# Output weights in 4 KB rows for four heads, and the last value load split in two, in a decode attention kernel

## The chip, the cores and the metric

The kernel runs on one core of one Trainium2 chip. The time is device microseconds of one execution, given as a median over runs. The profile is one execution recorded by the hardware profiler; its span (first to last instruction) is 1.5 to 1.9 us below the time. Landing times, start times and the durations of single DMA packets that the text quotes are records of the same traces.

## The reference, cut to what matters

Two attention layers decode one token for a batch of four; the results are put side by side. Part A has 8 key and value heads and looks at the last 2048 positions; part B has 32 heads and looks at the whole cache of 8192.

```python
def _B_ref(x, k_cache, v_cache, wq, wo):      # part A: the same, with a window and shared heads
    B, Sq, D = x.shape                        # 4, 1, 512
    H, Dh = 32, 128
    q = (x @ wq).reshape(B, Sq, H, Dh) ...    # transposed to heads
    scores = einsum("bhqd,bhkd->bhqk", q, k_cache) * Dh ** -0.5
    p = softmax(scores)
    o = einsum("bhqk,bhkd->bhqd", p, v_cache)
    return o ... .reshape(B, Sq, H * Dh) @ wo # wo: 4096 x 512, 4 MB in bf16
```

Keys and values of part B are 537 MB of the 587 that have to be read. Part B's output weights `wo` are only 4 MB.

## The kernel before: the parts that matter

Part B goes in 64 chunks: two heads of one batch element, 4 MB of keys and 4 MB of values. Each key tile is transposed on TensorE (into `tr`), copied to SBUF (`kt`), multiplied with the query (`sc`); the value tiles are multiplied with the probabilities (`po`). Two chunks are a "pair" here: their results are scaled (`oz`), brought into the row order of the weights by products with selection masks (into `ms`), cast (`zB`), and multiplied with the weights (`fin`).

The weights of two heads are one load, in rows of 2 KB, because partition p holds rows 2p and 2p+1:

```python
LASTV = (64, 32, 16, 8, 8)
...
def dma_wos(hp):
    src = B_wo[2 * hp * P:2 * (hp + 1) * P, :].rearrange("(p r) n -> p (r n)", r=2)
    sch.add_dma("sp", lambda e: e.dma_start(wos[:, :, :].rearrange("p r n -> p (r n)"), src), "d_wos",
                waits=[("fin", NCA + 4 * hp - 1)] if hp else [], key=("wos", hp))
```

The very last pair takes a shorter way from `po` to the result: its weights are turned back into plain row order beforehand, by products with `back2` masks, so that `oz` can be multiplied directly. The last chunk's values (128 tiles, 4 MB) arrive in pieces by `LASTV`:

```python
def emit_wol():
    for u in range(2):
        o = tr[:, u, :].bitcast(F32)
        for r in range(2):
            pe_mm(o, back2[:, u, r, :], wos[:, r, :], start=r == 0, stop=r == 1, ...)
        ...                                    # one copy on ScalarE, one on VectorE, into wol
...
norm_sum(NC - 1)                               # the end of the program
for g in range(chunks[NC - 1]["NG"]):
    emit_pv(NC - 1, g)                         # 8 value tiles each
    if g == LASTV[0] // TG - 1:
        emit_wol()                             # after the first 64 tiles
pv_done(NC - 1)
emit_fin(NC - 1)
```

## Time and profile before

| | before |
|---|---|
| time, median of 3 runs | 1374.14 us (1374.09 to 1374.22) |
| span of the profile | 1372.6 us |
| loads of part B's output weights | 16 of 256 KB, 2048 packets of 2 KB |
| values of the chunk before the last land at | 1359.160 us |
| last value load lands at | 1369.060 us |
| last value product starts at | 1369.326 us |

First, the end of the chain of work that ended last (start, duration, what). It says that the last value load was what TensorE waited for last:

```profile
1329.92 39.14 DMA kv<-in_B_v_cache_dram
1369.06 0.05 issue
1369.11 0.42 PE po L410 x8
```

Second, from the timeline, TensorE's wait (in brackets) for the values of the chunk before the last; third, from the table of waits, all its waits for part B's keys (sum in us, times, longest):

```profile
1359.21 0.64 PE L410 MATMUL po<-pbb,kv 128*128 128x64 bf16 x16 [0.46 <-DMA kv<-in_B_v_cache_dram]
```

```profile
PE tr L408 <- DMA kv<-in_B_k_cache_dram: 141.5, 58, 4.1
```

From 1359.21 on TensorE has work without a pause until the last pieces of the last chunk. So the stretch from the landing of those values to the last value product, 1369.326 - 1359.160 = 10.166 us, is a good measure of the end: what the queue gained or lost earlier does not enter into it. I call it **the end stretch** below. For everything ahead of it I use **the body**: from the landing of the very first load to the landing of those values, 1359.160 - 13.290 = 1345.870 us.

### The profile page before, as it was taken

What the parts mean: (1) busy time and instruction counts of PE and PEld (TensorE: products, weight loads), DVE (VectorE), ACT (ScalarE), POOL (GpSimd) and SP (SyncE); (2) the same over time, 40 slices, a digit from 0 to 9 for tenths busy, and PEclk for the clock granted to TensorE, in tenths of its full rate; (3) what the DMA queues carried; (4) which work ended last, traced back from release to release, by engine and by line L of the source; (5) the groups of instructions that cost most, each with busy time, mean ns of one, the idle gap of its engine ahead of it and who ended that gap; (6) DMA issues with size and microseconds to landing.
All of it is one profiled execution on the core that took longest, in us unless ns stands there. A gap on an engine that the chain in (4) does not pass through costs nothing.

```text
span 1372.6 us, 59967 instructions
## 1 busy us (share of the span) xinstructions
PE 1176.5 (86%) x27065; PEld 1132.9 (83%) x27067; DVE 656.6 (48%) x1434; ACT 434.7 (32%) x650; POOL 7.3 (1%) x28
## 2 busy tenths in 40 slices
PE   4888898889888888988888888888898888888888
PEld 4777898888888888888888878888898888888888
DVE  1775454445444444454445444444454444444544
ACT  1553232333223322332233323322333233323322
POOL 2000000000000000000000000000000000000000
PEclk9998999999999999999999999999999999999999
DMA  9999999999999999999999999999999999999998
GB/s 400 423 424 432 429 433 428 433 432 432 432 431 433 429 434 428 434 430 434 430 434 430 430 433 432 432 431 433 429 433 431 434 429 434 430 432 432 432 427 352
DMA packets 25261, 587.53 MB, mean 428 GB/s; under 512 B 2820, under 2 KB 2840, under 8 KB 6296
## 3 DMA queue, kind: packets, MB, share of 16 engines
q1 hardware_dynamic: 25208, 587.22, 99.8%
q8 instruction: 16, 0.26, 0.1%
q14 instruction: 5, 0.04, 0.0%
q10 hardware_dynamic: 32, 0.01, 0.0%
HBM read 587.21 MB, written 0.01 MB: 428 GB/s over the span
## 4 chain that ended last, share of the span: by engine, by line
DMA 65%; PE 33%; issue 1%; DVE 1%; ACT 0%; SPq 0%; DVEq 0%
DMA kv<-in_B_k_cache_dram 57%; PE tr L408 21%; PE sc L410 9%; DMA kv<-in_A_k_cache_dram 5%; DMA kv<-in_B_v_cache_dram 3%; PE po L410 2%; PE fin L410 1%; PE ms L410 0%; ACT kt L476 0%; DVE sA L527 0%; SPq L365 0%; ACT pba L597 0%; PE ms L408 0%; DVE zA L683 0%; DVE rm L536 0%
## 5 line engine op out<-in xcount | busy, mean ns | idle before, releaser
L408 PE MATMUL tr<-identb,kv 128*128 128x128 bf16 x8704 | 697.9, 230 | 148.8 <-DMA kv<-in_B_k_cache_dram 141.5
L478 DVE COPY kt<-tr 128x1024 bf16<-128x1024 bf16 x736 | 502.6, 690 | 457.1 <-PE tr L408 452.7
L408 PEld LDWEIGHTS tr<-identb,kv 128*128 128x128 bf16 x8704 | 552.9, 104 | 165.2 <-DMA kv<-in_B_k_cache_dram 81.7
L476 ACT ACTIVATE kt<-tr 128x1024 bf16<-128x1024 bf16 x352 | 359.3, 1023 | 666.8 <-PE tr L408 666.7
L410 PE MATMUL sc<-qb,kt 128*128 128x64 bf16 x8704 | 446.2, 196 | 14.3 <-ACT kt L476 12.8
L410 PEld LDWEIGHTS sc<-qb,kt 128*128 128x128 bf16 x8704 | 366.4, 100 | 26.0 <-ACT kt L476 20.2
L410 PE MATMUL po<-pbb,kv 128*128 128x64 bf16 x8320 | 284.4, 192 | 4.5 <-issue 3.9
L410 PEld LDWEIGHTS po<-pbb,kv 128*128 128x128 bf16 x8320 | 263.2, 97 | 7.1 <-issue 4.1
L577 ACT ACTIVATE pbb<-sc,negb 64x128 bf16<-64x128 f32 x128 | 51.6, 403 | 254.3 <-DVE negb L564 253.5
L541 DVE TENSOR_REDUCE rm<-sc 64x1 f32<-64x128 f32 x128 | 37.0, 289 | 56.6 <-PE sc L410 55.7
L553 DVE TENSOR_REDUCE gm<-ms 1x2 f32<-1x128 f32 (+1 forms) x72 | 20.1, 279 | 48.4 <-PE ms L408 48.4
L564 DVE COPY negb<-ms 128x1 f32<-128x1 f32 (+1 forms) x72 | 11.4, 158 | 47.0 <-PE ms L410 46.8
L410 PE MATMUL ms<-identf,gx 1*128 1x1 f32 (+1 forms) x144 | 27.2, 256 | 0.8 <-DVE zA L683 0.8
L666 DVE TENSOR_TENSOR oz<-po,rz 128x8 bf16<-128x8 f32 x33 | 5.5, 166 | 40.7 <-PE po L410 40.7
L410 PEld LDWEIGHTS ms<-identf,gx 1*128 1x128 f32 (+1 forms) x144 | 21.1, 182 | 4.6 <-DVE zA L683 0.9
L577 ACT ACTIVATION_READ_ACCUMULATOR pbb<-sc,negb 64x1 f32 x128 | 23.7, 185 | 0.0
L410 PE MATMUL po<-pba,kv 128*128 128x64 bf16 x512 | 20.5, 199 | 3.5 <-issue 2.1
L410 PEld LDWEIGHTS po<-pba,kv 128*128 128x128 bf16 x512 | 17.9, 102 | 5.7 <-ACT pba L597 4.2
L408 PE MATMUL ms<-identf,rm 128*1 128x128 f32 (+1 forms) x72 | 19.5, 271 | 2.4 <-DVE rm L536 2.3
L557 DVE TENSOR_SCALAR gx<-gm 1x128 f32<-1x128 f32 (+1 forms) x72 | 16.0, 222 | 2.5
L683 DVE CAST zB<-ms 64x8 bf16<-64x8 f32 x64 | 10.5, 164 | 9.2 <-PE ms L410 8.7
L410 PE MATMUL ms<-xT,kv 128*128 128x4 bf16 x256 | 7.1, 166 | 8.8 <-DMA kv<-in_A_wq_dram 5.0
(61 smaller groups left out, 173.9 us busy)
## 6 DMA issues: line engine op xcount, KB each, us to landing
kv<-in_B_k_cache_dram SPq DMA_DIRECT2D x63, 4096.0 KB, 26.5
kv<-in_B_v_cache_dram SPq DMA_DIRECT2D x63, 4096.0 KB, 30.9
kv<-in_A_k_cache_dram SPq DMA_DIRECT2D x8, 2048.0 KB, 14.8
kv<-in_A_v_cache_dram SPq DMA_DIRECT2D x8, 2048.0 KB, 16.2
kv<-in_A_wq_dram SPq DMA_DIRECT2D x1, 4096.0 KB, 12.5
kv<-in_B_wq_dram SPq DMA_DIRECT2D x1, 4096.0 KB, 27.1
wor<-in_A_wo_dram SPq DMA_DIRECT2D x8, 512.0 KB, 9.8
wos<-in_B_wo_dram SPq DMA_DIRECT2D x16, 256.0 KB, 20.3
```

Of the source, the lines that this page charges most:

```text
L408: sch.add("pe", lambda e: e.transpose(o, l, r), waits, key)
L410: sch.add("pe", lambda e: e.matmul(o, l, r, start=start, stop=stop), waits, key)
L476: sch.add("act", lambda e: e.activation(dst, src, ACTF.Copy), waits=waits, key=("ev", s))
L478: sch.add("dve", lambda e: e.tensor_copy(dst, src), waits=waits, key=("ev", s))
L541: sch.add("dve", lambda e, src=src, pp=pp: e.tensor_reduce(out=rm[pp, m, 0:1], in_=src, axis=AX.X, op=ALU.max), waits=[("S", ch["s_last"]) ...
L553: sch.add("dve", lambda e: e.tensor_reduce(out=gm[0:C, m, 0:U], in_=src, axis=AX.X, op=ALU.max), waits=[("trm", c)], key=("gmax", c))
L557: sch.add("dve", lambda e: e.tensor_scalar(out=dst, in0=gv, scalar1=-scale, scalar2=None, op0=ALU.mult), waits=[("gmax", c)], key=("gx", c))
L564: sch.add("dve", lambda e: e.tensor_copy(negb[:, m, 0:C], ms[:, col:col + C]), waits=[("bc", c)], key=("negb", c))
L577: sch.add("act", lambda e, src=src, pp=pp, n=n, u=u: e.activation(probs_of(c)[pp, :, u], src, ACTF.Exp, bias=negb[pp, m, 0:1], scale=scale ...
L666: sch.add("dve", lambda e: e.tensor_tensor(out=o, in0=i0, in1=i1, op=ALU.mult), waits=waits, key=("oT", c))
L683: sch.add("dve", lambda e, src=src, pp=pp: e.tensor_copy(z[pp, :].rearrange("p (r b) -> p r b", r=k), src), waits=[("sm", c)] + free if h ...
```

## The change

The intent: rows of 4 KB mean half as many packets for the weights, and half as many loads; with the last 256 KB of values in two loads, four value products instead of eight have to follow the very last landing. The price is that a load now serves four heads, that is two pairs of heads, so each pair's work runs over four rows per partition. The core of the diff (cut: comments, mask tables, loop constants, the places of the loads in the queue):

```diff
-LASTV = (64, 32, 16, 8, 8)
+LASTV = (64, 32, 16, 8, 4, 4)
...
-        def dma_wos(hp):
+        def dma_wos(hq):
-            src = B_wo[2 * hp * P:2 * (hp + 1) * P, :].rearrange("(p r) n -> p (r n)", r=2)
+            src = B_wo[4 * hq * P:4 * (hq + 1) * P, :].rearrange("(p r) n -> p (r n)", r=4)
...                                   # emit_sel
-            for r in range(k):                      # k = 2, n = 8 in part B
-                pe_mm(ms[:, Z0 + r * n:Z0 + (r + 1) * n], sel[:, r, :], x,
+            for r in range(4):
+                pe_mm(ms[:, Z0 + r * 16:Z0 + (r + 1) * 16], sel4[:, r, :], x,
...                                   # emit_wol
-                for r in range(2):
-                    pe_mm(o, back2[:, u, r, :], wos[:, r, :], start=r == 0, stop=r == 1,
+                for r in range(4):
+                    pe_mm(o, back4[:, u, r, :], wos[:, r, :], start=r == 0, stop=r == 3,
...                                   # emit_fin
-                ops = [(zB[:, r * NB:(r + 1) * NB], wos[:, r, :]) for r in range(2)]
+                ops = [(zB[:, r * NB:(r + 1) * NB], wos[:, r, :]) for r in range(4)]
```

More of the change, by code (lines that the diff above doesn't have):

```diff
@@ L216, in bass_concat_heads__sliding_block_cached__mha_block_cached__decode_kernel @@
         kt = sb("kt", [P, NKT, TG * P], BF16)
-        wos = sb("wos", [P, 2, DO], BF16)
+        wos = sb("wos", [P, 4, DO], BF16)
         qb = sb("qb", [P, 2, NW], BF16)
@@ L236, in bass_concat_heads__sliding_block_cached__mha_block_cached__decode_kernel @@
         rinv = sb("rinv", [P, NSM, 16], F32)
-        rz = sb("rz", [P, 8], F32)
-        pm = sb("pm", [P, HB // 2 + 1, 2, 2, 4], F32)
+        rz = sb("rz", [P, 16], F32)
+        pm = sb("pm", [P, HB + 2, 2, 2, 4], F32)
         pbt = {0: sb("pba", [P, NPB, NTA * 16 + NW], BF16), 1: sb("pbb", [P, NPB, NTB * 2 + NW], BF16)}
         oT = sb("oT", [P, NSM, 16], BF16)
-        oz = sb("oz", [P, 8], BF16)
+        oz = sb("oz", [P, 16], BF16)
         outsb = sb("outsb", [36, DO], BF16)
@@ L244, in bass_concat_heads__sliding_block_cached__mha_block_cached__decode_kernel @@
         sel4 = sb("sel4", [P, 4, P], BF16)
-        sel2 = sb("sel2", [P, 2, P], BF16)
-        back2 = sb("back2", [P, 2, 2, P], BF16)
+        back4 = sb("back4", [P, 2, 4, P], BF16)
         zA = sb("zA", [P, 2, 16], BF16)
-        zB = sb("zB", [P, 8], BF16)
+        zB = sb("zB", [P, 16], BF16)
         wol = sb("wol", [P, 2, DO], BF16)
@@ L279, in bass_concat_heads__sliding_block_cached__mha_block_cached__decode_kernel @@
         sch.add("pool", lambda e: e.memset(pm[:, :, :, :, :], 0.0), key="c_pm0")
-        for x in range(2):
-            sch.add("pool", lambda e, x=x: e.memset(pm[:, 1:, x, x, :], 1.0), waits=["c_pm0"], key="c_pm" if x else None)
+        for i in range(4):
+            sch.add("pool", lambda e, i=i: e.memset(pm[:, 2 + i::4, i // 2, i % 2, :], 1.0), waits=["c_pm0"], key="c_pm" if i == 3 else None)
         sch.add("pool", lambda e: e.memset(pbt[0][:, :, :], 0.0), key=("c_pb", 0))
@@ L290, in bass_concat_heads__sliding_block_cached__mha_block_cached__decode_kernel @@
                 fill=0.0, base=-r, channel_multiplier=1), waits=["c_onesb"])
-        for r in range(2):
-            sch.add("pool", lambda e, r=r: e.affine_select(
-                out=sel2[:, r, :], in_=onesb[:, :], pattern=[[0, 2], [-2, 64]], compare_op=ALU.is_equal,
-                fill=0.0, base=-r, channel_multiplier=1))
+        for r in range(4):
             for u in range(2):
                 sch.add("pool", lambda e, r=r, u=u: e.affine_select(
-                    out=back2[:, u, r, :], in_=onesb[:, :], pattern=[[1, P]], compare_op=ALU.is_equal,
-                    fill=0.0, base=P * u - r, channel_multiplier=-2), key="c_sel" if r == u == 1 else None)
+                    out=back4[:, u, r, :], in_=onesb[:, :], pattern=[[1, P]], compare_op=ALU.is_equal,
+                    fill=0.0, base=2 * P + P * u - r, channel_multiplier=-4), key="c_sel" if r == 3 and u == 1 else None)
         half_of = {}
@@ L334, in dma_wo @@
                         waits=[("fin", g - 2)] if g >= 2 and slot < 2 else [], key=("wo", g))
-        def dma_wos(hp):
-            src = B_wo[2 * hp * P:2 * (hp + 1) * P, :].rearrange("(p r) n -> p (r n)", r=2)
+        def dma_wos(hq):
+            src = B_wo[4 * hq * P:4 * (hq + 1) * P, :].rearrange("(p r) n -> p (r n)", r=4)
             sch.add_dma("sp", lambda e: e.dma_start(wos[:, :, :].rearrange("p r n -> p (r n)"), src), "d_wos",
-                        waits=[("fin", NCA + 4 * hp - 1)] if hp else [], key=("wos", hp))
+                        waits=[("fin", NCA + 8 * hq - 1)] if hq else [], key=("wos", hq))
         def dma_kv(kind, c):
@@ L387, in bass_concat_heads__sliding_block_cached__mha_block_cached__decode_kernel @@
         for kind, c in loads:
-            if kind == "k" and c >= NCA and (c == NCA or (c - NCA) % 4 == 3 and c > NCA + 3):
-                dma_wos((c - NCA) // 4)
+            if kind == "k" and c >= NCA and (c == NCA or (c - NCA) % 8 == 3 and c > NCA + 3):
+                dma_wos((c - NCA) // 8)
             dma_kv(kind, c)
             if kind == "v" and c > NCA and (c - NCA) % 2 == 1:
-                hp = max(0, c - NCA - 2) // 4
-                sch.add("sp", lambda e: e.sem_inc(sems["eng_sp"], 1), waits=[("wos", hp)] + (["kl"] if c == NC - 1 else []),
+                hq = max(0, c - NCA - 2) // 8
+                sch.add("sp", lambda e: e.sem_inc(sems["eng_sp"], 1), waits=[("wos", hq)] + (["kl"] if c == NC - 1 else []),
                         key=("wos2", c - 2 if c > NCA + 1 else NONE), self_inc=True)
@@ L398, in bass_concat_heads__sliding_block_cached__mha_block_cached__decode_kernel @@
                 dma_wo(c)
-        sch.add("sp", lambda e: e.sem_inc(sems["eng_sp"], 1), waits=[("wos", HB // 2 - 1)], key=("wos2", NC - 1), self_inc=True)
+        sch.add("sp", lambda e: e.sem_inc(sems["eng_sp"], 1), waits=[("wos", HB // 4 - 1)], key=("wos2", NC - 1), self_inc=True)
         ms_read = []
@@ L646, in norm_sum @@
             if c >= NCA or c == NONE:
-                pair = 4 * (c - NCA - 1 + 4) if c != NONE else 8
+                pair = 16 * ((c - NCA - 1) // 2 + 2) if c != NONE else 16
                 pv = pm[:, :, :, :, :].rearrange("p a b c d -> p (a b c d)")
                 sch.add("dve", lambda e, x=0: e.tensor_tensor(
-                    out=rz[:, :].rearrange("p (x y) -> p x y", x=2), in0=bcast(ri, [[0, 2], [1, 4]]),
-                    in1=pv[:, bass.ds(x + pair, 8)].rearrange("p (x y) -> p x y", x=2), op=ALU.mult),
+                    out=rz[:, :].rearrange("p (x y) -> p x y", x=4), in0=bcast(ri, [[0, 4], [1, 4]]),
+                    in1=pv[:, bass.ds(x + pair, 16)].rearrange("p (x y) -> p x y", x=4), op=ALU.mult),
                     waits=[("rinv", c), "c_pm"], key=("rz", c), at=pair)
@@ L661, in norm_out @@
             else:
-                o, i0 = oz[:, :].rearrange("p (x y) -> p x y", x=2), bcast(po[:, 0:4], [[0, 2], [1, 4]])
-                i1 = rz[:, :].rearrange("p (x y) -> p x y", x=2)
+                o, i0 = oz[:, :].rearrange("p (x y) -> p x y", x=4), bcast(po[:, 0:4], [[0, 4], [1, 4]])
+                i1 = rz[:, :].rearrange("p (x y) -> p x y", x=4)
             waits = [("rinv" if 0 <= c < NCA else "rz", c), ("pv", c)] + ([("sm", c - 2 if c != NCA + 1 else NONE)] if c >= 2 else [])
@@ L671, in emit_sel @@
             if 0 <= c < NCA:
-                sel, x, n, z, k = sel4, oT[:, c % NSM, :], 16, zA[:, c % 2, :], 4
+                x, z, order = oT[:, c % NSM, :], zA[:, c % 2, :], "p (r b h) -> p h r b"
                 free = [("fin", c - 2)] if c >= 2 else []
             else:
-                sel, x, n, z, k = sel2, oz[:, :], 8, zB[:, :], 2
+                x, z, order = oz[:, :], zB[:, :], "p (r s b u) -> p s u r b"
                 free = [("fin", c - 2 if c - 2 >= NCA else NONE)] if c != NONE else []
-            for r in range(k):
-                pe_mm(ms[:, Z0 + r * n:Z0 + (r + 1) * n], sel[:, r, :], x,
-                      waits=[("oT", c)] + ms_read if r == 0 else [], key=("sm", c) if r == k - 1 else None)
-            for h in range(k):
-                pp = slice(h * P // k, (h + 1) * P // k)
-                src = ms[pp, Z0:Z0 + k * n].rearrange("p (r b h) -> p h r b", r=k, b=NB)[:, h]
-                sch.add("dve", lambda e, src=src, pp=pp: e.tensor_copy(z[pp, :].rearrange("p (r b) -> p r b", r=k), src),
-                        waits=[("sm", c)] + free if h == 0 else [], key=("z", c) if h == k - 1 else None)
+            for r in range(4):
+                pe_mm(ms[:, Z0 + r * 16:Z0 + (r + 1) * 16], sel4[:, r, :], x,
+                      waits=[("oT", c)] + ms_read if r == 0 else [], key=("sm", c) if r == 3 else None)
+            for h in range(4):
+                pp = slice(h * P // 4, (h + 1) * P // 4)
+                if 0 <= c < NCA:
+                    src = ms[pp, Z0:Z0 + 64].rearrange(order, r=4, b=NB)[:, h]
+                else:
+                    src = ms[pp, Z0:Z0 + 64].rearrange(order, r=4, s=2, b=NB)[:, h // 2, h % 2]
+                sch.add("dve", lambda e, src=src, pp=pp: e.tensor_copy(z[pp, :].rearrange("p (r b) -> p r b", r=4), src),
+                        waits=[("sm", c)] + free if h == 0 else [], key=("z", c) if h == 3 else None)
             ms_read[:] = [("z", c)]
@@ L690, in emit_wol @@
                 o = tr[:, u, :].bitcast(F32)
-                for r in range(2):
-                    pe_mm(o, back2[:, u, r, :], wos[:, r, :], start=r == 0, stop=r == 1,
-                          waits=[("wos2", NC - 1)] if u == r == 0 else [], key=("back", u) if r else None)
+                for r in range(4):
+                    pe_mm(o, back4[:, u, r, :], wos[:, r, :], start=r == 0, stop=r == 3,
+                          waits=[("wos2", NC - 1)] if u == r == 0 else [], key=("back", u) if r == 3 else None)
                 if u == 0:
@@ L701, in emit_fin @@
             if c == NC - 1:
-                ov = oz[:, :].rearrange("p (b u) -> p b u", u=2)
+                ov = oz[:, 8:16].rearrange("p (b u) -> p b u", u=2)
                 ops = [(ov[:, :, u], wol[:, u, :]) for u in range(2)]
```

## The prediction

> **What bounds the kernel now.** I read the page first, for the busy shares and the DMA row; then the queue and issue tables; then the chain of work that ended last, in the steady part; then the end of the timeline.
>
> ```profile
> PE 1176.5 (86%) x27065; PEld 1132.9 (83%) x27067; DVE 656.6 (48%) x1434; ACT 434.7 (32%) x650; POOL 7.3 (1%) x28
> DMA  9999999999999999999999999999999999999998
> DMA packets 25261, 587.53 MB, mean 428 GB/s; under 512 B 2820, under 2 KB 2840, under 8 KB 6296
> q1 hardware_dynamic: 25208, 587.22, 99.8%
> ...
> DMA 65%; PE 33%; issue 1%; DVE 1%; ACT 0%; SPq 0%; DVEq 0%
> ...
> wor<-in_A_wo_dram SPq DMA_DIRECT2D x8, 512.0 KB, 9.8
> wos<-in_B_wo_dram SPq DMA_DIRECT2D x16, 256.0 KB, 20.3
> ```
>
> The load queue's packets fill 99.8% of the 16 engines' span. No engine of the core comes near that: TensorE is next at 86%. So what the kernel can win in its body is queue time: fewer bytes (this change removes none) or less time per byte. The packet line says where time per byte may be lost: 587 MB go in 25261 packets, but 6296 of them are under 8 KB.
>
> ```profile
> 341.26 27.88 DMA kv<-in_B_k_cache_dram
> 369.19 1.51 PE tr L408 x24
> ...
> 380.11 28.58 DMA kv<-in_B_k_cache_dram
> 408.75 1.51 PE tr L408 x24
> ...
> 419.67 27.89 DMA kv<-in_B_k_cache_dram
> 447.60 1.51 PE tr L408 x24
> ```
>
> Columns: start, duration, what. Key tiles that the chain follows arrive at 369.19, 408.75 and 447.60: periods of 39.56 and 38.85 us. Each has four 4 MB loads; the longer one has one load of output weights (256 KB) more. That load therefore costs about 0.70 us of the queue. Also, a key load lands 26 to 28 us after its issue while the queue takes 9.7 us for 4 MB (16.78 MB in 38.85 us): at each issue nearly two loads are still ahead of it. Compute that gets later by well under 10 us does not empty the queue.
>
> The end of the timeline (start, duration, engine, line, operation, idle before it in brackets):
>
> ```profile
> 1364.10 2.05 PE L410 MATMUL po<-pbb,kv 128*128 128x64 bf16 x64
> ...
> 1366.20 0.81 PE L410 MATMUL tr<-wos,back 128*128 128x512 bf16 x3
> ...
> 1366.85 2.03 PE L410 MATMUL po<-pbb,kv 128*128 128x64 bf16 x56
> ...
> 1369.11 0.41 PE L410 MATMUL po<-pbb,kv 128*128 128x64 bf16 x8 [0.23 <-DMA kv<-in_B_v_cache_dram]
> 1369.62 0.17 DVE L666 TENSOR_TENSOR oz<-po,rz 128x8 bf16<-128x8 f32 x1 [1.88 <-PE po L410]
> 1369.84 0.38 PE L410 MATMUL fin<-wol,oz 128*4 128x256 bf16 x4 [0.33 <-DVE oz L666]
> 1370.27 0.42 DVE L724 CAST outB<-fin 68x256 bf16<-68x256 f32 x1 [0.48 <-PE fin L410]
> ```
>
> The last eight value products wait for the last load, but only 0.23 us by this view. TensorE is nearly as late as the queue at the end. That small margin decides this case.
>
> **What the Trainium skill says.** "DMA: Bandwidth & Descriptors", section "Why small descriptors are slow (HBM only)", names a fixed overhead per packet and 32 bytes of descriptor metadata per operation. The trace agrees that there is a fixed part. Its packet records on the load queue have these means: 2 KB 84.6 ns, 4 KB 161.4, 16 KB 616.4, 32 KB 1218.3. The two ends give a line of 0.0369 ns per byte and about 9 ns per packet. The same page, section "Where 436 GB/s comes from", puts the fabric's ceiling at 435.2 GB/s. The slices of the page move 428 to 434, so long rows leave nothing to win. "TensorE: Matmul & The Clock Gate", section "Back-to-back issue gap", gives N/2.4 + 2.5 ns, 216 ns at 512 columns. The start times of the three recorded products into tr are 215 ns apart: the trace agrees. "VectorE: DVE Perf Modes", section on the TRN2 errata, says that short operations pay a fixed cost. Here the casts of 64x8 take 164 ns and those of 32x16 in the sliding-window part 170, so more columns are nearly free, and more instructions are not.
>
> **The change part by part.**
>
> (1) Output weights: 16 loads of 256 KB in 2 KB rows become 8 of 512 KB in 4 KB rows. By packets: 2048 x 84.6 = 173.3 us of engine time become 1024 x 161.4 = 165.3; the difference over 16 engines is 0.50 us. Each load also ends in 16 packets of 4 bytes at 9.1 ns, one per engine; eight loads fewer save 8 x 9.1 ns = 0.07. Sum 0.57. By landings: a wos load lands 0.672 us (median of 16) after the load ahead of it, while the 512 KB loads of wor, which already have 4 KB rows, take 1.253 (median of 8). Per 512 KB that is 2 x 0.672 - 1.253 = 0.091 us, and 0.73 for eight. I choose 0.65 in between. All of it is queue time, and the queue is the bound, so everything after should shift by that: the value tile before the last, which landed at 1359.16, lands at about 1358.5.
>
> (2) Each pair of chunks gets more to do. There are 32 pairs. Selection: four products of 128x16 for two of 128x8. Casts into zB: four of 32x16 for two of 64x8, 4 x 0.170 - 2 x 0.164 = +0.35 us of VectorE. Products with wos: eight for four, about +0.3 us of TensorE (the chain has 0.31 for four). Over 32 pairs TensorE gets some 12 us and VectorE 11. TensorE stood idle for key loads for 141.5 us, 58 times, in the table of waits; these 0.4 us per pair lie in that. Worth 0 on the path. GpSimd builds two masks more (0.29 us each) during the first 10 us, before anybody needs them: 0.
>
> (3) The queue's tail. The last 256 KB, 2 KB rows in one load, become two of 128 KB in 1 KB rows. From the line above a 1 KB packet takes about 47 ns; eight per engine, twice, are 0.75 us against 8 x 84.6 = 0.68, plus 9 ns for another completion: +0.08 us. The last landing moves from 1369.06 by -0.65 + 0.08 to about 1368.49. If the landing still released the end, four products instead of eight would follow it, at 29 ns apart: another -0.12, and the total would be -0.69.
>
> (4) TensorE's tail. The last pair's weights are turned round by products of the back masks with wos, after the first 64 value tiles: four of 512 columns before, eight after. That adds 4 x 0.215 = +0.86 us, in the one stretch where TensorE has no margin. I follow its records there. It starts the value products of the chunk before when that chunk's values land (1359.16), and runs without a gap until 1367.76. From then on it stands still for 0.04, 0.16 and 0.39 us, ahead of the last three pieces (start to start, less the usual 29 ns), 0.59 in all. So the last value product, which started at 1369.326, starts at 1369.326 - 0.65 (earlier landing of the values before) + 0.86 - 0.59 (waits eaten up) = 1368.95. With the landing alone it could have started at 1368.49 + 0.05 + 3 x 0.03 = 1368.63. TensorE is the later of the two by some 0.3 us.
>
> (5) After that nothing changes in length: scaling into oz (twice as wide, same 0.17 us), four final products, the cast, the store.
>
> Sum: -0.65 + 0.86 - 0.59 = -0.38 us. I allow 0.04 for passing the extra waits on semaphores: -0.34, so 1373.8 us from 1374.14. The span of the profile goes from 1372.6 to about 1372.3.
>
> **The rivals.** First, that the queue still ends the kernel: -0.7 us, 1373.45. For it speaks that the margin, 0.3 us, is of the size of the uncertainty of (1); against it that the extra products alone, 0.86, exceed all 0.59 us of waits. The other way round, TensorE could be late already on arriving at the values before the last: it waited 0.46 us for them (at 1359.2), and (2) takes about 0.4 of that. If casts also hold up an eviction, another 0.2 us are lost: 1374.0. Third, that bigger weights loads cost what they save: a 512 KB load is in front of the first key tile of the full-cache part instead of 256 KB, and makes that tile 0.6 us later, where the queue is less deep; or 4 KB rows gain only 0.25 us. For that speaks the tail, where 256 KB in 2 KB rows land in 0.640 us and 512 KB in 4 KB rows in 1.249, only 0.03 apart per 512 KB. Then the tail's products are uncovered: -0.25 + 0.86 - 0.59 = 0.0, 1374.2. Fourth, that a slower TensorE starves the queue: some 0.4 us per pair times 32, +13 us. Against it stand the waits of TensorE and the two loads in the queue ahead; I give it one chance in 100.
>
> **Range and chances.** The rivals that I take seriously lie between 1373.45 and 1374.2, and the runs before lay within 0.13 us. I widen it a little for another chip: 1373.2 to 1374.5 holds it 8 times in 10. Two per cent are 27 us, and nothing here is near that: faster 0.005, within 2% 0.985, slower 0.01.
>
> **What would show it.** (1) The page should have 8 loads of wos with 512 KB each, some 1000 packets fewer (25261 - 1024 - 128 + 128 + 16 = 24253), and long periods of the chain should come every eight chunks, with about 1.26 us more than the short ones. The values before the last should land at about 1358.5. (2) 256 products of fin with wos, 128 casts into zB, TensorE's wait for keys less by 10 us or so, the queue's share still 99.8%. (4) Eight products into tr with wos, about 1.7 us long; the value products after them in one run with no idle time ended by a load; the chain's last DMA piece no longer the last value load but the one before. If TensorE still waits for the last load, the first rival is true; if the values before the last land before 1358.3 or after 1358.8, (1) was sized wrong; if TensorE starts on them more than 0.2 us after they land, (2) was not hidden.

## The result, and the profile after

The changed kernel took 1373.94 us (median of five, 1373.47 to 1374.80), the kernel before 1374.22 us in five runs (1374.09 to 1374.29). The ratio is 0.9999 with a 95% interval of 0.9984 to 1.0013: the same time. (Ratios are the mean time of one kernel's fast runs over that of the other's of the same rounds, so not quite the ratio of the medians.)

The page of the changed kernel: the busy line, the packets, the load queue, and the loads of weights.

```profile
PE 1184.8 (86%) x27261; PEld 1140.6 (83%) x27263; DVE 665.1 (48%) x1498; ACT 435.2 (32%) x650; POOL 8.2 (1%) x32
DMA packets 24252, 587.52 MB, mean 428 GB/s; under 512 B 2708, under 2 KB 2984, under 8 KB 5288
q1 hardware_dynamic: 24200, 587.22, 99.7%
wos<-in_B_wo_dram SPq DMA_DIRECT2D x8, 512.0 KB, 20.9
```

A thousand packets fewer, the same bytes, and the queue is as full as before. The chain of work that ended last, in the steady part (start, duration, what; the landing is the sum of the two numbers):

```profile
343.93 25.50 DMA kv<-in_B_k_cache_dram
382.17 26.12 DMA kv<-in_B_k_cache_dram
422.01 25.14 DMA kv<-in_B_k_cache_dram
459.93 27.36 DMA kv<-in_B_k_cache_dram
500.79 25.36 DMA kv<-in_B_k_cache_dram
```

Landings at 369.43, 408.29, 447.15, 487.29 and 526.15: three periods of 38.86 us and one of 40.14. The weights now come once in four periods and cost 1.28 us, where they cost 0.70 us in every second period. The end of the same chain:

```profile
1328.71 29.78 DMA kv<-in_B_v_cache_dram
1358.49 0.05 issue
1358.54 0.65 PE po L407 x16
...
1363.53 1.96 PE po L407 x64
1365.48 0.05 issue
1365.53 1.67 PE tr L407 x7
1367.21 1.89 PE po L407 x64
```

This is the change that the reader should see: the chain's last DMA piece is no longer the last value load but the values of the chunk before, landing at 1358.49. From there on it is TensorE all the way. The products with the back masks take 1.67 us (one of the eight records is missing) and the 64 value products after them run in one piece, with no wait. The last load had landed at 1368.424; the last value product started at 1368.889. The two waits that answer to those shown of before:

```profile
1358.54 0.65 PE L407 MATMUL po<-pbb,kv 128*128 128x64 bf16 x16 [0.19 <-DMA kv<-in_B_v_cache_dram]
```

```profile
PE tr L405 <- DMA kv<-in_B_k_cache_dram: 134.9, 59, 4.7
```

TensorE's pause before the last values but one has shrunk from 0.46 to 0.19 us, and its waits for keys by 6.6 us. Both fit the extra pair work: the pause is 0.44 and 0.46 us in the two traces with the old pair work (before, e3) and 0.18 to 0.21 in the nine others in which that work is not doubled in the late pairs.

So far everything looks as predicted: those values landed 0.669 us earlier than before. But 0.294 us of that was there from the beginning, since the first load landed at 12.996 instead of 13.290. The body went from 1345.870 to 1345.495 us only. One trace is not enough to size term (1).

### The profile page after: what moved, and what is told of

The parts are those of the page before. It is cut to its first block, busy times and chain, and to the rows that moved or that the text cites. A ratio compares the mean times of both kernels' runs of the same rounds, so it can differ in the third digit from the quotient of the medians.

```text
span 1372.3 us, 60420 instructions
## 1 busy us (share of the span) xinstructions
PE 1184.8 (86%) x27261; PEld 1140.6 (83%) x27263; DVE 665.1 (48%) x1498; ACT 435.2 (32%) x650; POOL 8.2 (1%) x32
## 4 chain that ended last, share of the span: by engine, by line
DMA 59%; PE 38%; DVE 1%; issue 1%; ACT 1%; SPq 0%; DVEq 0%
DMA kv<-in_B_k_cache_dram 55%; PE tr L405 23%; PE sc L407 9%; PE po L407 3%; DMA kv<-in_B_v_cache_dram 2%; DMA kv<-in_B_wq_dram 2%; PE fin L407 2%; PE ms L407 1%; DVE sA L524 1%; ACT kt L473 0%; DVE rm L533 0%; DVE sA L522 0%; PE ms L405 0%; ACT pba L594 0%; PE tr L407 0%
## 5 line engine op out<-in xcount | busy, mean ns | idle before, releaser
L405 PE MATMUL tr<-identb,kv 128*128 128x128 bf16 x8704 | 697.0, 230 | 137.7 <-DMA kv<-in_B_k_cache_dram 134.9
L683 DVE CAST zB<-ms 32x16 bf16<-32x16 f32 x128 | 21.8, 170 | 11.1 <-PE ms L407 9.8
L663 DVE TENSOR_TENSOR oz<-po,rz 128x16 bf16<-128x16 f32 x33 | 5.8, 175 | 40.3 <-PE po L407 40.3
L407 PEld LDWEIGHTS po<-pba,kv 128*128 128x128 bf16 x512 | 17.9, 102 | 5.4 <-ACT pba L594 4.2
L407 PE MATMUL fin<-wos,zB 128*4 128x256 bf16 x256 | 19.3, 272 | 0.0
```

The source lines that it names most:

```text
L405: sch.add("pe", lambda e: e.transpose(o, l, r), waits, key)
L407: sch.add("pe", lambda e: e.matmul(o, l, r, start=start, stop=stop), waits, key)
L663: sch.add("dve", lambda e: e.tensor_tensor(out=o, in0=i0, in1=i1, op=ALU.mult), waits=waits, key=("oT", c))
L683: sch.add("dve", lambda e, src=src, pp=pp: e.tensor_copy(z[pp, :].rearrange("p (r b) -> p r b", r=4), src), waits=[("sm", c)] + free if h ...
```

## The experiments

All numbers in one table; the text takes them up. "Body" and "end stretch" are as defined above; "last landing" is that of the last value load, counted like the end stretch from the landing of the chunk before's values.

| kernel | median (range) us, runs | body us | last landing us | end stretch us |
|---|---|---|---|---|
| before | 1374.14 (1374.09-1374.22), 3 | 1345.870 | 9.900 | 10.166 |
| changed | 1373.94 (1373.47-1374.80), 5 | 1345.495 | 9.933 | 10.398 |
| e1: changed, again | 1373.80 (1373.66-1373.97), 5 | 1345.331 | 9.951 | 10.401 |
| e2: rows only | 1373.80 (1373.46-1373.95), 5 | 1345.238 | 9.916 | 10.394 |
| e3: split only | 1374.17 (1373.93-1374.36), 5 | 1345.801 | 9.935 | 10.083 |
| e4: narrow back products | 1373.38 (1373.21-1374.36), 5 | 1345.143 | 9.937 | 10.085 |
| e5: 512 KB in 2 KB rows | 1374.19 (1374.13-1374.29), 4 | 1345.588 | 9.948 | 10.387 |
| e6: back products twice | 1375.54 (1375.22-1376.49), 4 | 1345.180 | 9.944 | 12.135 |
| e7: pair work twice | 1375.54 (1374.20-1377.34), 4 | 1346.678 | 9.939 | 10.837 |
| e8: narrow, no split | 1373.41 (1373.28-1373.59), 4 | 1345.343 | 9.904 | 10.168 |
| e9: pair work twice, late pairs | 1375.69 (1375.53-1375.88), 5 | 1346.872 | 9.886 | 10.831 |
| e10: pair work twice, early pairs | 1375.14 (1375.08-1376.53), 5 | 1346.632 | 9.916 | 10.390 |
| e11: narrow, again | 1373.37 (1373.29-1374.21), 5 | 1345.039 | 9.952 | 10.100 |

Beside these the kernel before was run again: medians 1374.07 us (e1 to e4, 9 runs), 1374.07 (e5 to e8, 7) and 1374.13 (e9 to e11, 9). The three groups ran on three different chips. By the ratio each of these kernels counts as the same as the kernel before (every 95% interval contains 1.000): effects this small are not decided by that ratio. What follows rests on stretches of the traces, and on medians only where they lie well apart.

**The theory** is that of the prediction: a gain of about half a microsecond of queue time in the body, by fewer packets, and at the end a loss on TensorE, which has 0.86 us more to do than before and only 0.6 us of waits to do it in. **The rivals**: the queue bounds the end too; the gain comes from the number of loads; the trace showed luck; a slower TensorE costs queue time; the chips differ.

### e1: the changed kernel again

No edit.

> The changed kernel once more, unaltered, to learn how far one trace and one set of runs can be trusted: the traced gain of 0.3 us is smaller than the 1.3 us between the fastest and slowest of its first five runs. Theory (weights gain 0.5 us of queue, TensorE's tail takes part of it back): wos loads again land 1.275 us after the load before them, the values before the last land within 0.3 us of 1358.49, no idle time ended by a load after the products with the back masks, span 1371.9 to 1372.7. Rival (what the first trace showed was luck of the start, where the first load landed 0.29 us earlier than in the kernel before): with a start like that of the kernel before, the values before the last land at about 1358.8.

The first load landed at 13.282 us this time, as late as in the kernel before, and the values before the last still landed at 1358.613, 0.55 us earlier than before. A load of weights again landed 1.27 us after the load ahead of it. The first trace's early start was luck; the gain was not, but it is smaller than 0.67. The end stretch came out at 10.401, 3 ns from the first trace: this measure is good to some hundredths.

### e2 and e3: one part of the change each

e2 is the changed kernel without the split, e3 the kernel before with the split alone:

```diff
# e2, on the changed kernel
-LASTV = (64, 32, 16, 8, 4, 4)
+LASTV = (64, 32, 16, 8, 8)
# e3, on the kernel before
-LASTV = (64, 32, 16, 8, 8)
+LASTV = (64, 32, 16, 8, 4, 4)
```

> 4 KB rows of the output weights alone; last 256 KB of values in one load as in the kernel before. Theory (TensorE is the later one at the end): the last load lands at about 1368.4 (0.638 after the one before it), some 0.2 us before TensorE comes to its eight tiles, so nothing waits for it and the last value product follows the landing of the values before the last by the same 10.40 us (1368.89 minus 1358.49) as with the split; the split is worth 0.00 to 0.03 us. Rival (the queue sets the end, and the split pays): the last eight products wait for the load, and the end is 0.1 us or more later than with the split, measured from the landing of the values before the last.

> The kernel before with only the last 256 KB of values split in two. Its TensorE waits 0.39 us longer than usual for the last load. Theory: the split lets four of the eight products run inside that wait, the last load lands 0.02 to 0.08 us later, the last four products follow it, so the last value product starts about 10.06 us after the landing of the values before the last, where it took 10.17 (1369.326 minus 1359.160): a gain of about 0.1 us, with idle time ended by the last load left in the trace. Rival (1 KB rows cost more than they save): 10.17 or more.

With the weights in 4 KB rows the split is worth nothing: 10.394 us without it, 10.398 and 10.401 with it. With the weights in 2 KB rows it is worth 10.166 - 10.083 = 0.08 us, though the load in two parts is complete 0.035 us later (9.900 to 9.935). That is the signature of a changed bound: in the kernel before TensorE waits for the last load and gains when less work follows it; in the changed kernel it comes later than the load. The rows cost the end stretch 10.394 - 10.166 = 0.23 us. The split's saving is swallowed.

### e4 and e11: the back products made cheap

The last pair uses the weights of the last two of four heads, which lie in partitions 64 to 127; half `u` of the result comes from 32 partitions alone. So the products can be cut to these, and the two halves sent in turn, to different rows of the array and different banks:

```diff
-            for u in range(2):
-                o = tr[:, u, :].bitcast(F32)
-                for r in range(4):
-                    pe_mm(o, back4[:, u, r, :], wos[:, r, :], start=r == 0, stop=r == 3, ...)
+            for r in range(4):
+                for u in range(2):
+                    pp = slice(64 + 32 * u, 96 + 32 * u)
+                    pe_mm(tr[:, u, :].bitcast(F32), back4[pp, u, r, :], wos[pp, r, :], start=r == 0, stop=r == 3, ...)
```

> The changed kernel, with the products that turn the last weights cut to the 32 partitions that hold the rows of each, and sent in pairs to different partitions and different banks. Same result. Theory (TensorE's 1.7 us of such products are the bound at the end): if the pairs overlap, eight products take about 0.86 us, TensorE gets 0.86 earlier to the last tiles, waits again for the last load, and the last value product starts 0.14 us after that load lands: 10.07 us after the values before the last instead of 10.40, so 0.33 us faster than the changed kernel, span about 1372.0, time about 1373.6. Rival one (the pairs do not overlap): 10.40 and no change. Rival two (the queue was the bound all along): no change either, but then with the products at 0.86 us.

> The kernel with narrow, paired back products a second time, unaltered, as the best version so far: 1373.38 median with one run at 1374.36 among five. Theory: the last value product starts 10.08 us after the values before the last land, median 1373.2 to 1373.6, below the 1373.8 of the changed kernel and the 1374.07 of the kernel before. Rival (its gain was a lucky set): 1373.8.

The timeline of e4, back products and the value products after them:

```profile
1365.23 1.03 PE L407 MATMUL tr<-wos,back 32*128 32x512 bf16 x8
1366.20 2.39 PE L407 MATMUL po<-pbb,kv 128*128 128x64 bf16 x64
```

All eight take 1.03 us from the first start to the last end, three steps of 0.22 us and the 0.37 us of the last; the two products of a pair start 3 to 5 ns apart, so the pairs overlap. The 64 value products are spread over 2.39 us, where the same view of e6, below, has 2.03 for them without any wait: they wait for pieces again, in short waits that this view merges. The end stretch is 10.085 and 10.100, that is 0.31 us less than in the changed kernel, and the last product starts 0.15 us after the last landing (0.14 expected). Both sets have the lowest medians, 1373.38 and 1373.37. This kernel computes the right result and is, with e8 below, the fastest: 0.7 us below the kernel before, though each of its two sets has one late run (1374.36 and 1374.21). The interval of the ratio (0.9996, 0.9982 to 1.0010 in e11) cannot separate 0.05%; for the difference speak the traces and two equal medians.

### e6: the back products doubled

```diff
-                for r in range(4):
-                    pe_mm(o, back4[:, u, r, :], wos[:, r, :], start=r == 0, stop=r == 3, ...)
+                for i, r in enumerate([0, 1, 2, 3] * 2):
+                    pe_mm(o, back4[:, u, r, :], wos[:, r, :], start=r == 0, stop=r == 3, ...)
```

> The changed kernel with the eight products with the back masks sent twice over (the second pass starts the sums afresh, same result). Theory (TensorE's work after the landing of the values before the last sets the end, one for one): eight products more at 0.2155 us are 1.72, so the last value product starts 12.12 us after that landing instead of 10.40, and the time is 1.7 us more than the changed kernel's, about 1375.6. Rival (TensorE still has slack there): clearly less than 1.7, with waits shrinking.

```profile
1365.55 3.40 PE L407 MATMUL tr<-wos,back 128*128 128x512 bf16 x15
1368.79 2.03 PE L407 MATMUL po<-pbb,kv 128*128 128x64 bf16 x64
```

The end stretch grew by 12.135 - 10.401 = 1.73 us for eight products of 0.2155, and the time by 1.74 (1375.54 against 1373.80 of e1). In the changed kernel this work is on the path one for one. Together with e4 that settles which engine is the later one at the end.

### e8: the split where TensorE is no longer late

e4's kernel with `LASTV = (64, 32, 16, 8, 8)`.

> The kernel with the narrow, paired back products, but the last 256 KB of values in one load again. Theory (the split pays only where TensorE waits for the last load, as it does here): the last load lands 9.92 us after the values before the last, eight products follow, the last starts at 10.17 instead of 10.085: the split is worth 0.08 us here, where it was worth 0.00 beside the wide products. Rival (the split never matters): 10.085.

```profile
1366.21 1.84 PE L407 MATMUL po<-pbb,kv 128*128 128x64 bf16 x56
1368.28 0.41 PE L407 MATMUL po<-pbb,kv 128*128 128x64 bf16 x8 [0.23 <-DMA kv<-in_B_v_cache_dram]
```

The wait of the kernel before is back, 0.23 us, and the end stretch is 10.168: the split is worth 0.08 us again. Whether a part of a change pays was decided by another part of it. In the medians (1373.41 against 1373.38) so small a gain is not to be seen.

### e5: rows or number of loads

The same eight loads of 512 KB, but in 256 rows of 2 KB. The rows then lie wrongly in SBUF, so the result is wrong (relative error 0.48).

```diff
-            src = B_wo[4 * hq * P:4 * (hq + 1) * P, :].rearrange("(p r) n -> p (r n)", r=4)
-            ... wos[:, :, :].rearrange("p r n -> p (r n)"), src
+            src = B_wo[4 * hq * P:4 * (hq + 1) * P, :].rearrange("(s p r) n -> p s (r n)", s=2, r=2)
+            ... wos[:, :, :].rearrange("p (s r) n -> p s (r n)", s=2), src
```

> The changed kernel with the same eight 512 KB loads of output weights, each in 256 rows of 2 KB instead of 128 of 4 KB (the rows then lie wrongly, so the full-cache half of the result is wrong on purpose). Theory (the queue's gain comes from the rows, by a fixed time per packet): a load takes 256 x 84.6 / 16 = 1.354 us of an engine instead of 128 x 161.6 / 16 = 1.293, and lands 1.33 us after the one before it instead of 1.275; from the first landing to the values before the last 1345.7 us instead of 1345.3 (mean of four traces with 4 KB rows: 1345.14 to 1345.50), as in the traces with 2 KB rows (1345.80 and 1345.87) within 0.2. Rival (the gain is that of eight loads instead of sixteen): 1.275 and 1345.3.

A load landed 1.344 us after the one ahead of it (median of eight; 1.275 with 4 KB rows): twice the 0.672 of a 256 KB load before is 1.344 too. So the rows make the difference, about as 256 packets of 84.6 ns against 128 of 161.6 over 16 engines say (1.354 and 1.293 us; in e5 itself the 2 KB packets took 86.6 ns on average), and the rival with the number of loads falls. The body was 1345.588. With that, the three traces with 2 KB rows have bodies of 1345.59, 1345.80 and 1345.87 (mean 1345.75). The seven with 4 KB rows and normal pair work have 1345.04 to 1345.50 (mean 1345.25). The gain in the body is 0.50 us, with single traces up to 0.25 us from their mean. It is not one between chips: on one chip e3 lies 0.56 us above the mean of e1, e2 and e4, on another e5 0.33 above that of e6 and e8.

### e7, e9, e10: is the pair work free?

e7 doubles the extra work of each pair without changing the result: selection products twice, casts twice (first into a spare tile `zC`), eight more products against zeros. e9 does so only from the fifth pair on, e10 only before.

```diff
+            twice = 1 if 0 <= c < NCA else 2    # e9: 2 if c >= NCA + 9 else 1;  e10: the first ones
-            for r in range(4):
+            for i, r in enumerate(list(range(4)) * twice):
...
-            for h in range(4):
+            for i, h in enumerate(list(range(4)) * twice):
...
-                ops = [(zB[:, r * NB:(r + 1) * NB], wos[:, r, :]) for r in range(4)]
+                nil = pbt[1][:, 1, NTB * 2:NTB * 2 + NB]
+                ops = [(nil, wos[:, r, :]) for r in range(4)] + [(zB[:, r * NB:(r + 1) * NB], wos[:, r, :]) for r in range(4)]
```

> The changed kernel with the pair work of the full-cache part doubled: selection products sent twice, casts made twice (the first pass into a spare tile), eight more products with the weights against zeros. Same result. That adds some 1.0 us of TensorE (8 x 0.104 and four small ones) and 0.68 of VectorE to each of 32 pairs, 31 us of TensorE in all. Theory (that work lies in TensorE's waits for key loads, except in the last pair): from the first landing to the values before the last still 1345.3 within 0.2, TensorE's wait for keys smaller by some 30 us (134.9 before), and only at the end TensorE comes late to the values before the last: its 0.19 us of waiting is gone and the last value product starts about 10.40 + 0.8 = 11.2 us after that landing; time 0.8 more than the changed kernel's, 1374.6. Rival (a slower TensorE releases key buffers later and starves the queue): several us more, and the queue's share under 99%.

> Doubled pair work again, but only from the fifth pair on; the first pairs of the full-cache part as in the changed kernel. In the run with all pairs doubled the queue lost 1.1 us against the changed kernel, 0.9 of it between 160 and 195 us, where a load of 4 MB landed only 13.5 to 14 us after its issue (28 later on), so that less than one and a half loads were queued. Theory (pair work is free where two or more loads are queued, and costs only at the shallow start of the full-cache part): from the first landing to the values before the last 1345.3 within 0.25, and the last value product 10.84 us after that landing as with all pairs doubled; time about 1374.3. Rival (slower pairs cost queue time anywhere): 1346.2 or more.

> The other half: pair work doubled in the first five emissions only (up to about 250 us). Theory: the queue loses about 0.9 us before 200 us and nothing after, so from the first landing to the values before the last 1346.2, and the end after that landing as in the changed kernel (10.40); time about 1374.7. Rival: 1345.3 here, and the loss in the run with only the late pairs doubled.

In e7 TensorE's waits for keys went from 134.9 to 109.6 us, so the work did go into them; and the end stretch grew by 0.44 us (10.837, expected 11.2): after the last pair that has this work, TensorE found only the pause of 0.19 us to lose, and began on the values before the last 0.55 us after their landing instead of 0.05. But the body grew by 1.35 us against e1's, and this I had not expected: the time came to 1375.54, not 1374.6. Compared landing by landing with e1, it lost 1.1 us in two steps before 194 us and one of 0.24 at 477, and nothing anywhere else. So I formed a second theory: part B starts with a shallow queue, and there the extra work costs. e10 refutes it as stated: with the early pairs doubled, its landings are 0.28 us ahead of e1's at 124 us and still 0.26 ahead at 320. The same stretches of e7 and e10 (bounds and length, then busy time of PE, PEld, DVE, ACT and POOL, then TensorE's granted clock, DMA share, GB/s):

```profile
156.00:164.00 8.00, 6.51 (x173) 6.14 (x170) 3.13 (x7) 2.05 (x2) 0.00 (x0) 1.00 0.97 397
164.00:172.00 8.00, 5.29 (x91) 5.12 (x92) 1.53 (x4) 1.25 (x5) 0.00 (x0) 0.79 1.04 426
172.00:180.00 8.00, 8.00 (x189) 8.00 (x187) 5.64 (x11) 3.75 (x4) 0.00 (x0) 1.00 0.95 397
```

```profile
156.00:164.00 8.00, 5.61 (x160) 5.30 (x157) 2.06 (x7) 1.71 (x5) 0.00 (x0) 0.98 1.03 440
164.00:172.00 8.00, 8.00 (x150) 8.00 (x148) 4.34 (x8) 2.64 (x4) 0.00 (x0) 0.81 0.98 420
172.00:180.00 8.00, 7.80 (x213) 7.62 (x210) 4.50 (x9) 2.51 (x3) 0.00 (x0) 1.00 1.02 438
```

In e7 the queue moves only 397 GB/s in two of the stretches, and TensorE is busy for 5.29 of 8 us between them. A load lands there 13.5 to 14.1 us after its issue, against 15.2 to 17.9 in e1 and 17.1 to 19.1 in e10: it was issued later than usual, so there was less in the queue. e10 had more work in the same place and no loss. So this loss does not come with the early work every time, and e7's four runs, 1374.20, 1375.40, 1375.68 and 1377.34, say that it differs from run to run: the first of them has none, the last about 3 us. What triggers it was not found. It is thus not excluded that more pair work makes such losses more frequent; one of e10's five runs, 1376.53, was late too.

e9 and e10 lost 1.5 us each at another place, between the landings at 320 and 350 us, and this is most likely an artefact of the edit: where the pair work changes, TensorE's program gets a third loop (a line of the edit that is not shown provides for it). The part of the DMA view for 314 to 356 us of e9 (queue, packets, MB, share of 16 engines):

```profile
q1 hardware_dynamic: 739, 17.86, 99.4%
q8 instruction: 6, 0.10, 1.0%
```

Six instruction packets of 16 KB, about 1.08 us of a DMA engine each, stand there among the loads; e10 has six there as well, and none of the eleven other traces has one between 175 and 1366 us. That these packets cost the time was not tested by itself: the loss comes with the first three, and the last two cost nothing. After it, e9's late pairs cost nothing: from the landing at 350.216 in e1 (351.715 in e9) to the values before the last it is 1008.40 us in e1 and 1008.29 in e9. The end stretch was as expected in both: 10.831 with the last pair doubled, 10.390 with it not. So doubled pair work is free in the steady part and costs 0.44 us at the end. The body of e9 as a whole, 1346.872, is where the rival had put it (1346.2 or more), but all of the loss lies at the loop and none after it. My expectation for the time of e9 (1374.3, measured 1375.69) was off by what was lost there. That for e10 (1374.7, measured 1375.14) was off by that loss one way and by the early loss that did not come the other way.

## Why the prediction was right, point by point

The predicted 1373.8 us and the measured 1373.94 agree, and the end came about in the predicted way. The two effects measured over all traces, 0.50 us gained in the body and 0.23 lost at the end, make 0.27, and the medians differ by 0.27 (e1 against its runs of the kernel before) and 0.28 (the result). Term by term:

- **(1) The weights, -0.65 us.** The kind was right, the size 0.15 us too large. The traces give -0.50 (means of seven and three). The prediction had two workings, 0.57 from packets and 0.73 from landings, and chose between them. The second borrowed 1.253 us for a 512 KB load from part A's loads (the median of these eight is rather 1.259); the new loads landed 1.275 after the one ahead, which alone makes 0.55 of the 0.73. Nor is the gap of the 2 KB loads a constant: 0.672 us in the trace before, 0.653 in e3. The packet sum was the better one. That the values landed at 1358.49 as predicted was in part the luck of a start 0.29 us early.
- **(2) The pair work, 0 on the path.** Right in the steady part, even when doubled. It took 0.27 us of the 0.46 that TensorE waited before the last values but one, so the second rival had a point but did not come true. TensorE's busy time grew by 8.3 us and VectorE's by 8.5, where 12 and 11 were worked out, and TensorE's waits for keys shrank by 6.6 us, not by 10 or more.
- **(3) The split, +0.08 us on the last landing.** It measured +0.033 in this pair of traces and 0.035 in e3. A packet of 1 KB took 46.5 ns against the 47 worked out; but loads in the tail land faster than the sum of their packets' durations, and those in two parts more so: 0.638 us where that sum is 0.69 for the one load, 0.662 where it is 0.76 for the two.
- **(4) TensorE's end, +0.86 - 0.59.** Right: the end stretch grew by 0.232 us, of 0.27 worked out and 0.31 with the allowance. e4 and e6 show that the 0.86 are real and on the path, e2 and e8 that the waits eaten up are those for the last pieces.
- **(5) Nothing after that changes.** Right up to the store, which is issued 0.43 us earlier (1370.29 against 1370.72). The predicted sum for the last value product was -0.38, it moved by -0.437. The span shrank by only 0.25: from the last value product to the span's end it took 3.42 us in this trace and 3.23 in the one before, and the difference lies in the last records after the store, where the engines wait for each other. This goes with the change: it is 3.41 to 3.43 us in the nine traces that have both the loads for four heads and the split, and 3.22 to 3.24 in the four that lack one of them (before, e2, e3, e8); why was not looked into. The time does not follow it: from the last value product to the end of the time of the profiled execution it is 4.95 to 5.10 us in all thirteen, and the times of the two profiled executions, 1374.43 and 1373.95 us, differ by 0.48.
- **The rivals.** That the queue still ends the kernel fell with e2 and e6. That the bigger load loses at the start of part B did not show: its first key tile landed 0.32 us later than before (0.62 counted from the first load, which is what the larger weights load in front of it takes), and from the third landing on the distance stays 0.32 until the next load of weights. That 4 KB rows gain only 0.25 us is half of what the bodies show. A starved queue did not come about in the changed kernel's traces. One of its ten runs took 1374.80, which the kernel before did not reach in any run. It is not alone: of the 51 runs of kernels with the pair work over four rows, six lie 0.8 us or more above the median of their set (one each of the changed kernel, e4, e6, e7, e10 and e11), of the 35 of the kernel before and e3 none lies over 0.3 above. So the change may cost an occasional late run; e7 shows that such a thing can happen early in part B, but no trace of a late run of the changed kernel itself was caught. That stays open.
- **Readings.** "The slices of the page move 428 to 434" GB/s holds for 35 of the 40; the first three and the last two are lower (352 to 427). In the Trainium skill, "TensorE: Matmul & The Clock Gate", section "Back-to-back issue gap", gives its 216 ns for an isolated product, and some 131 ns for products in a stream with weight loads; the products with the back masks, each with its weight load, start 215 to 216 ns apart here. The section on the TRN2 errata of "VectorE: DVE Perf Modes" is mainly about operations that read SBUF; the casts into zB read PSUM, for which its table has a fixed term as well.

## What to carry to other kernels

In this kernel, bound by a full queue, longer rows paid about what the packet durations say (0.57 us worked out, 0.50 measured), and the place to check what they cost is the end, where the other engines have few waits left to hide work in. Work that is free for a thousand microseconds can cost time in the last ten (0.44 us for the doubled pair work, all 1.73 for the doubled back products): list the waits after the last-but-one landing, add up the new work there, and compare. If the new work is larger, make it cheaper or move it, as the narrow products do here; then the other half of the change begins to pay too (0.08 us of the end stretch here, too little to be seen in the times).

## What the Trainium skill lacked or had wrong

- "DMA: Bandwidth & Descriptors", the table of specifications, gives 512 bytes or more as enough for line rate. In a full queue the runs show a clear slope above that: packets of 1 KB take 46.5 ns (22 bytes per ns), 2 KB 84.6 (24), 4 KB 161.6 (25), 32 KB 1218 (27). No page has such a list of packet durations.
- The same page, section "Rules for kernel authors", asks for 1 MiB or more per DMA for the most bandwidth. Behind other loads in the queue, 256 KB loads landed 0.672 us after the one ahead of them, which is 390 GB/s, and 512 KB loads in 4 KB rows 1.275 us, which is 411; the large ones move 432. The length of the row, not of the load, made most of this difference (512 KB in 2 KB rows: 1.344 us).
- "Runtime: NRT & Kernel Launch", section "Instruction fetch mechanics", calls the cost of crossing a 16 KiB block of instructions mostly hidden; of branches it says that they can stall the engine. It says nothing of the loads that share the DMA engines with these fetches. In e9 and e10 one loop more brought six such packets of about 1.08 us, and over the first three of them the key and value loads fell 1.5 us behind for good. That the packets were the cause was not tested by itself.
